# A latest start in the planner for conversions and operands that a one-core Trainium2 kernel makes ahead

## Chip, core and metric

The kernel runs on one core of one Trainium2 chip. The metric is the device time of one execution in microseconds; lower is better. Before the change the median of three runs is 877.93 us (876.68 to 880.76).

## What is computed

A layer of attention with a sigmoid in place of the softmax, followed by two feed-forward blocks. The shapes are 4 x 12 heads of 448 x 64, 1792 tokens, model width 768, and inner widths 768 and 2048.

```python
def _attn_ref(q, k, v):                  # (4, 12, 448, 64)
    scores = scale * np.matmul(q, k.transpose(0, 1, 3, 2)) - np.log(S)
    attn = 1.0 / (1.0 + np.exp(-scores))
    return np.matmul(attn, v).astype(np.float32)

def _moe_ref(x, w1, w2, w3, w_out):      # x: 1792 x 768, all weights 768 x 768
    h = np.maximum(np.maximum(x @ w1, x @ w2), x @ w3)
    return (h @ w_out).astype(np.float32)

def _moe2_ref(x, w_in, w_out):           # w_in 768 x 2048, w_out 2048 x 768
    h = x @ w_in
    g = h * (1.0 / (1.0 + np.exp(-1.702 * h)))
    return (g @ w_out).astype(np.float32)
```

All products run in float32 precision, and the weights arrive as 64-bit floats, which the kernel itself turns into 32-bit ones.

## The kernel before

**Stages, in order of TensorE's work.** Attention over 24 pairs of heads ("couples"), in twelve double steps; the first feed-forward block for tokens of two batches at a time, as layer 1 (first pass), layer 2 (first pass), layer 1 (second pass, the other two batches), layer 2 (second pass); then the second block, in groups of its inner width (`tp, fp`, lines 886 to 901), and a tail.

**Products.** A 2 x 2 block product is done with seven products in place of eight (the sums of blocks are made in `moving` for the activations and in `Weights.steps` for the weights; `Set.step` places the seven). Each factor is split into a rounded part and a rest (`split`, line 382: a cast and a subtraction), and a product of 384 in depth is three blocks times three matmuls: nine matmuls of 448 columns, `product`, line 484, issued at line 492. The planner counts 9 x 0.201 us for it. A `stage` (line 536) runs the sets of a layer interlocked, 9 x 7 = 63 steps in layer 1 and 3 x 7 in layer 2.

**Weights, and what is made ahead.**
- `single` (line 346) turns one 128 x 768 tile of 64-bit weights into 32-bit ones: a load of 768 KB (line 353), on ScalarE L357 (the high word) and L362 (the low bits; in attention this part is on VectorE, L364), on VectorE L367, L368 and L372. The raw words go into one of two places, `raw_at`, in turn (some take a third place); the result into one of four places, `y_at`.
- `prepare` (line 665) and `prepare4` (line 671) call it long before the tile is used and write the result to DRAM (`yk`, `y4`). 18 are declared in attention (`convert`, line 679), 6 beside the first pass of layer 1, 16 beside the second pass, and 16 beside the first four groups of the second block (lines 896 to 900): 56 in all.
- `Weights.operand` (line 469) makes one operand of a product: at its first use it is split from the 32-bit tile into a slot of a ring of nine (`w_at`) and written to DRAM (`kept`); later uses load it from `kept`. In the second pass of layer 1 four of the nine sets (`REDO`) make their operands anew.
- The list `extra` (lines 773 to 783) holds what the second pass of layer 1 does beside its own work, 24 pieces: 8 `prepare`, 8 `prepare4`, and for the first pair of tiles of the second block a reload of `yk` (`Weights(12, ...)`) and its seven operands, each with a split and a write to `kept`. Their order is: tile pair 12 (two), the reload, seven operands, two `prepare4`, then four conversions for each of the next three pairs. `stage` declares piece j after step floor(63j/24) + 1.

**What sets the order of work.** Nothing runs where it is written. Every operation is declared to `Order` (line 88) with the places in memory that it reads and writes, so its predecessors follow; `Order.run` (line 126) then makes a plan on the host and issues the instructions in that order on TensorE, VectorE, ScalarE and SP (which issues all DMAs). On the chip each engine takes its instructions strictly as issued, and semaphores hold them.

The planner has two passes. Backward, each operation gets `late`, the latest start that delays nobody: the smallest `late` of its successors minus its own cost and a lag (0.1 us, after a DMA 1.0 us, after a raw load 2.0 us). TensorE's operations have a fixed `at`: `O.clock`, the sum of TensorE's planned work that was declared before them. Forward, each engine that is free takes, of the operations that are ready, the one with the smallest `late`:

```python
            late = min((x.late - took - o.lag for x in o.post), default=1e9)
            o.late = late if o.at is None else min(late, o.at)
...
                heapq.heappush(ready[e], (o.late + (SLACK if e == "DVE" and len(o.on) > 1 else 0.0), o.n, o))
```

Planned costs are those of lines 48 to 57 (768 columns: 0.84 us on ScalarE, 0.96 or 0.56 us on VectorE), 1.95 us for L362, and for a DMA its size over 350 KB/us plus 2.0 us and the lag. A conversion, whose reader is a reload far behind, so has a `late` that can lie far behind the place where it is declared; its only other bounds are the buffers it shares with later work.

Of the kernel before, what the change touches and what calls it, by code (L numbers as in the profile page):

```python
# [186 lines left out]
T = S  # L187
# [12 lines left out]
EARLY = 4  # L200
LEAD = 2
READY = 1
REDO = (1, 3, 5, 7)


def moe_chain_kernel(tc, qk, vv, wa, wb, out):
# [3 lines left out]
    O = Order()  # L210
# [36 lines left out]
    def F(at, n):  # L247
        if at >= FAR2:
            return Reg(sn4, at - FAR2, n, lambda: slab_n[3][:, at - FAR2 : at - FAR2 + n])
        if at >= FAR:  # L250
            return Reg(sn1, at - FAR, n, lambda: slab_n[0][:, at - FAR : at - FAR + n])
        return Reg(sf, at, n, lambda: slab_f[:, at : at + n])
# [38 lines left out]
    def dma(to, of, kb, reads=None, writes=None):  # L291
        return O.op(
            {"SP": kb / BUS},
            lambda e: sp.dma_start(to().bitcast(F32), of().bitcast(F32)),
            [of] if reads is None else reads,
            [to] if writes is None else writes,
        )
# [27 lines left out]
    XA, XB = 0, FAR  # L325
# [24 lines left out]
    def single(of, y, low_on, at=None, after=()):  # L350
        at = raw_at() if at is None else at
        raw = F(at, 2 * DM)
        O.op({"SP": 768 / BUS}, lambda e: sp.dma_start(raw().bitcast(mybir.dt.uint64), of), (), [raw], after, lag=LAND_RAW)
        half = lambda n: words(raw(), U16, n)
        u = lambda: y().bitcast(U32)
        by = dict(op0=ALU.bitwise_and, op1=ALU.bitwise_or)
        on("ACT", t_act(DM), lambda: act.activation(y(), words(raw(), F32, 1), AF.Copy, scale=2.0**-112), [raw], [y])  # L357
        byte = lambda: words(raw(), U8, 4)

        def low(e):  # L360
            if e == "ACT":
                act.activation(byte(), words(raw(), U32, 0), AF.Copy, scale=LOW)  # L362
            else:
                dve.tensor_scalar(half(2), half(1), 13, None, op0=ALU.logical_shift_right)  # L364

        O.op({low_on: 1.95 if low_on == "ACT" else 1.02}, lambda _: low(low_on), [raw], [raw])
        on("DVE", t_one(DM), lambda: dve.tensor_scalar(y(), y(), -TOP, TOP, op0=ALU.max, op1=ALU.min), [y], [y])  # L367
        on("DVE", t_one(DM), lambda: dve.tensor_scalar(u(), u(), 3, None, op0=ALU.logical_shift_left), [y], [y])  # L368
        on(
            "DVE",  # L370
            t_two(DM),
            lambda: dve.scalar_tensor_tensor(u(), words(raw(), U32, 1), 0x80000007, u(), **by),  # L372
            [y, raw],
            [y],
        )
# [49 lines left out]
    def tensors(i):  # L425

        if i < 9:
            return [(wa, 3 * m + i % 3) for m in (i // 3, i // 3 + 3)]
        if i < 12:
            return [(wa, 18 + m) for m in (i - 9, i - 6)]  # L430
        return [(wb, 4 * (i - 12) + n) for n in range(2)]
# [52 lines left out]
    def product(ps, w, x, fresh):  # L484
# [15 lines left out]

        O.pe(f, 9 * MM, [*w, *(z for p in parts for z in p)] + ([] if fresh else [ps]), [ps])

    def temp():
        return F(temp_at(), T)

    class Set:


        def __init__(self, x, weights, put, bank, temp=temp):
            self.x, self.weights, self.put, self.bank, self.temp = x, weights, put, bank, temp  # L510
# [25 lines left out]
    def stage(sets, extra=()):  # L536
        steps = sorted((7 * i + 2 * n, i, n) for i in range(len(sets)) for n in range(7))
        done = 0
        for k, (_, s, n) in enumerate(steps):
            sets[s].step(n)  # L540
            while done * len(steps) < (k + 1) * len(extra):
                extra[done]()
                done += 1


# [119 lines left out]
    def prepare(i, n, low="DVE", at=None, after=()):  # L665
        of, t = tensors(i)[n]
        y = F(y_at() if at is None else at + 2 * DM, DM)
        single(of[t], y, low, at, after)
        dma(yk[i][1](n), y, 384)

    def prepare4(f, low):
        y = F(y_at(), DM)
        single(wb[tile4(f)], y, low)
        dma(y4[f], y, 384)

    def tile4(f):
        return f % 8 * 4 + 2 + f // 8

    def convert(c):
        p = c.p - LEAD  # L680
        if 0 <= p < 18:
            prepare(p // 2, p % 2, at=XA + 12 * T if c.p % 3 == 2 else None, after=[c.load])

    prev, last = None, None
    for i in range(NP // 2):
        x = Couple(2 * i)
        x.values()
        if i == 0:
            x.score(0, slice(0, 1))
            x.score(1, slice(0, 1))  # L690
            x.score(0, slice(1, 3))
            x.scored(0)
            x.score(1, slice(1, 3))
            x.scored(1)
        for n in range(0 if i else 2, 3):
            x.score(n)
            x.scored(n)
        convert(x)
        if prev:
            weigh_last(prev, last)  # L700
        y = Couple(2 * i + 1)
        y.values()
        last = sigmoid(score_last((x, y)))
        for n in range(3 if prev else 0):
            prev[1].weigh(n)
        for n in range(3):
            y.score(n)
            y.scored(n)
        convert(y)
        for n in range(3):  # L710
            x.weigh(n)
        prev = (x, y)
# [12 lines left out]
    def layer1(x, first, base, extra=()):  # L725
        sets = []
        for m in range(HK):
            for e in range(3):

                def put(half, tok, ps, other, m=m, e=e):  # L730
                    to = pairs(base, half, tok, m)
                    if e == 0 and other is None:
                        copy(to, ps, S, psum=True)
                        return
                    if other is not None:
                        new = to if e == 0 else temp()
                        add(new, ps, other, S)
                        ps = new
                    if e:
                        two(to, ps, to, ALU.max, S)  # L740

                def weights(i=3 * m + e):
                    if first or i not in REDO:
                        return Weights(i, first, sums(), keep=i not in REDO)
                    at = again()
                    return Weights(i, True, at + 2 * DM, y=at, keep=False)

                sets.append(Set(x, weights, put, ps_at))
        stage(sets, extra)
# [3 lines left out]
    def layer2(h, first, base):  # L753
        sets = []
        for m in range(HK):

            def put(half, tok, ps, other, m=m):
                to = temp() if base is None else pairs(base, half, tok, m)
                if other is None:
                    copy(to, ps, S, psum=True)  # L760
                else:
                    add(to, ps, other, S)
                dma(zk[base is not None][half][tok][1](m), to, 224)

            sets.append(Set(h, lambda m=m: Weights(9 + m, first, sums()), put, ps_at))
        stage(sets)
# [6 lines left out]
    extra = []  # L773
    for fp in range(EARLY):
        for n in range(2):
            extra.append(lambda fp=fp, n=n: prepare(12 + fp, n, "ACT"))
        if fp < READY:
            w = []
# [22 lines left out]
    class Group:  # L801


        def __init__(self, fp, tp, z):
            self.fp, self.tp, self.g, self.w = fp, tp, {}, None
            first = self.first = (tp == 1) == (fp < PAIRS // 2)
            early = self.early = fp < EARLY or fp >= PAIRS // 2
            self.set = Set(z, lambda: Weights(12 + fp, first and fp >= READY, s3, early), self.put, b3)
            self.at = None
# [68 lines left out]
    half = PAIRS // 2  # L878

    def reload(tp):  # L880
        for side in range(2):
            for tok in range(2):
                dma(F(raw0 + (6 * side + 3 * tok) * T, 3 * T), zk[tp][side][tok][0], 672)
        return moving(raw0, t=s3, at=zslots)
# [3 lines left out]
    for tp, fp in [(1, n) for n in range(half)] + [(0, n) for n in range(PAIRS)]:  # L888
        if (tp, fp) == (0, 0):
            z = reload(0)  # L890
        g = Group(fp, tp, z)
        for n in range(7):
            g.set.step(n)
            for i in range(2 * n - 2, 2 * n) if before and n else ():
                before.unit(i)
        if tp == 0 and fp < half:
            for n in range(2):
                prepare(12 + half + fp, n, "ACT")
            for n in range(2):
                prepare4(half + fp + 8 * n, "ACT")  # L900
        before = g


# [11 lines left out]
    def put3(half, tok, ps, other, k):  # L915
        g = F(G[2 * half + tok] + k * T, T)
        if other is not None:
# [4 lines left out]
        two(g, ps, sg, ALU.mult, S)  # L922

    stage(
        [
            Set(
# [205 lines left out]
```

## Time and profile before

| | |
|---|---|
| median of three runs | 877.93 us |
| profiled execution, its own time | 878.68 us |
| its span in the profile | 876.5 us |
| granted TensorE clock | full speed in all 40 slices |
| TensorE matmul, busy | 864.5 us (99%), 4558 instructions |
| weight loads, busy | 747.7 us (85%) |
| VectorE, busy | 690.0 us (79%), 1107 instructions |
| ScalarE, busy | 503.0 us (57%), 731 instructions |
| DMA | 238.13 MB, 272 GB/s in the mean |

How to read it: the profiler's span is that of one execution, and the execution's own time is 2.2 us longer. PE is TensorE, PEld its weight loads, DVE VectorE, ACT ScalarE, SP the engine that issues DMAs (SPq is its queue). The names of tiles are the program's: f, n, m and r are the four slabs of on-chip memory, ps the accumulators, yk, y, kept, z and spill are in DRAM, in_wb and in_wa are the raw weights. `f<-in_wb` reads "f is written from in_wb". Ends of matmuls are modelled by the profiler, so the waits of the weight loads tell more of TensorE's holes than its busy time. Planned times (`O.clock`, `late`) are the planner's own and not times of the device.

### The profile page before, as it was taken

Reading aid. Unit: us, or ns where it says so; the run is one execution under the profiler, and the core shown is the slowest. Engines: PE = TensorE matmul, PEld = TensorE weight load, DVE = VectorE, ACT = ScalarE, POOL = GpSimd, SP = SyncE. Lnnn points to the kernel's source line nnn. Section 1 sums busy time; section 2 is a strip of 40 time slices with the busy share of each in tenths; the row PEclk is TensorE's granted clock in tenths of the full one; section 3 lists DMA queues with packets and bytes.
Section 4 is the critical chain, followed back from the end, with each engine's and each line's share of the span. In section 5 each row is a group of like instructions: output and inputs, shape, how many; then the busy total and the mean of one; then the engine's idle time right before and its main releaser. Section 6 shows DMA issues by size and latency. Waiting matters only on the chain.

```text
span 876.5 us, 12583 instructions
## 1 busy us (share of the span) xinstructions
PE 864.5 (99%) x4558; PEld 747.7 (85%) x4558; DVE 690.0 (79%) x1107; ACT 503.0 (57%) x731; POOL 1.1 (0%) x6
## 2 busy tenths in 40 slices
PE   9999999999999989999999999999999999999998
PEld 5544448999998978999989999999999999999997
DVE  5888898878899877778697888756688888753894
ACT  7887887556566545566566444665665444423540
POOL 0000000000000000000000000000000000000000
PEclk9999999999999999999999999999999999999999
DMA  8899977777839988888989956998768674686113
GB/s 300 299 317 326 373 248 240 248 257 248 290 153 375 366 314 298 277 298 297 395 349 385 367 167 196 388 354 321 276 247 303 251 276 148 217 283 199 31 64 126
DMA packets 77533, 238.13 MB, mean 272 GB/s; under 512 B 8608, under 2 KB 18208, under 8 KB 77472
## 3 DMA queue, kind: packets, MB, share of 16 engines
q1 hardware_dynamic: 77472, 237.34, 76.5%
q8 instruction: 36, 0.59, 0.2%
q14 instruction: 25, 0.20, 0.1%
HBM read 151.19 MB, written 86.11 MB: 271 GB/s over the span
## 4 chain that ended last, share of the span: by engine, by line
PE 94%; DVE 4%; DMA 1%; ACT 1%; issue 1%; POOLq 0%; DVEq 0%; POOL 0%; ACTq 0%
PE ps L492 53%; PE ps L859 7%; PE ps L858 7%; PE ps L860 7%; PE ps L602 7%; PE ps L1000 6%; PE ps L583 6%; DVE f L312 2%; DVE r L312 1%; PE ps L646 1%; PE ps L635 1%; DMA kept<-r 1%; PE ps L662 0%; DVE m L312 0%; ACT r L309 0%
## 5 line engine op out<-in xcount | busy, mean ns | idle before, releaser
L492 PE MATMUL ps<-r 128*128 128x448 f32 x2250 | 465.8, 362 | 4.2 <-DVE f L312 2.3
L492 PEld LDWEIGHTS ps<-r 128*128 128x128 f32 x2250 | 421.3, 188 | 35.6 <-DVE f L312 1.9
L312 DVE TENSOR_TENSOR f<-ps,f 128x448 f32<-128x448 f32 x214 | 132.5, 623 | 90.8 <-PE ps L860 35.4
L312 DVE TENSOR_TENSOR r<-f,r 128x384 fp32r<-128x384 f32 (+3 forms) x252 | 160.7, 660 | 11.2 <-ACT r L309 10.1
L309 ACT CAST r<-f 128x384 fp32r<-128x384 f32 (+3 forms) x206 | 113.7, 580 | 66.0 <-PE ps L492 30.5
L309 ACT COPY f<-ps 128x448 f32<-128x448 f32 x124 | 66.5, 540 | 109.5 <-PE ps L492 75.8
L312 DVE TENSOR_TENSOR f<-f 128x384 f32<-128x384 f32 (+2 forms) x189 | 121.3, 659 | 9.1 <-ACT f L921 4.1
L618 ACT ACTIVATE m<-ps,bias 128x896 f32<-128x896 f32 x84 | 78.8, 1007 | 11.4 <-PE ps L583 10.0
L362 ACT ACTIVATE f<-f 128x768 uint8<-128x768 uint32 x38 | 74.8, 1968 | 0.6
L357 ACT ACTIVATE f<-f 128x768 f32<-128x768 f32 x56 | 51.2, 915 | 17.7 <-DMA f<-in_wb 9.5
L492 PE MATMUL ps<-m,r 128*128 128x448 f32 x270 | 58.4, 363 | 1.4 <-DVE r L309 1.1
L602 PE MATMUL ps<-m,f 128*64 128x448 f32 x288 | 59.4, 548 | 0.0
L372 DVE SCALAR_TENSOR_TENSOR f<-f 128x768 uint32<-128x768 uint32 x56 | 53.2, 954 | 4.9 <-ACT f L362 4.4
L583 PEld LDWEIGHTS ps<-r 64*128 64x128 f32 x432 | 39.3, 187 | 19.1 <-ACT m L618 9.2
L492 PEld LDWEIGHTS ps<-m,r 128*128 128x128 f32 x270 | 50.4, 187 | 5.7 <-DVE r L309 1.5
L583 PE MATMUL ps<-r 64*128 64x448 f32 x432 | 50.7, 376 | 0.0
L602 PEld LDWEIGHTS ps<-m,f 128*64 128x64 f32 x288 | 18.5, 136 | 34.4 <-issue 31.7
L309 ACT COPY ps<-ps 128x448 f32<-128x448 f32 x43 | 23.2, 539 | 31.9 <-PE ps L492 28.8
L309 ACT CAST m<-f 128x448 fp32r<-128x448 f32 (+4 forms) x36 | 26.1, 724 | 23.9 <-DVE f L312 15.8
L312 DVE TENSOR_TENSOR n<-f,n 128x448 fp32r<-128x448 f32 (+4 forms) x51 | 37.9, 745 | 1.7 <-ACT n L309 1.1
L367 DVE TENSOR_SCALAR f<-f 128x768 f32<-128x768 f32 x56 | 31.1, 555 | 8.2 <-ACT f L357 8.0
L312 DVE TENSOR_TENSOR m<-f,m 128x448 fp32r<-128x448 f32 (+4 forms) x41 | 34.0, 832 | 4.1 <-ACT m L309 4.0
(81 smaller groups left out, 896.1 us busy)
## 6 DMA issues: line engine op xcount, KB each, us to landing
r<-kept SPq DMA_DIRECT2D x119, 384.0 KB, 4.9
kept<-r SPq DMA_DIRECT2D x112, 384.0 KB, 5.2
f<-in_wb SPq DMA_DIRECT2D x32, 768.0 KB, 7.1
f<-in_wa SPq DMA_DIRECT2D x24, 768.0 KB, 6.9
f<-yk SPq DMA_DIRECT2D x24, 768.0 KB, 5.5
yk<-f SPq DMA_DIRECT2D x40, 384.0 KB, 6.8
f<-y SPq DMA_DIRECT2D x24, 384.0 KB, 5.4
f<-in_qk SPq DMA_DIRECT2D x15, 456.0 KB, 5.8
```

The source lines that it names most:

```text
L309: return O.op(engines, lambda e: (act.copy if e == "ACT" else dve.tensor_copy)(to(), of()), [of], [to])
L312: return on("DVE", t_two(n), lambda: dve.tensor_tensor(to(), a(), b(), op=op), [a, b], [to])
L362: act.activation(byte(), words(raw(), U32, 0), AF.Copy, scale=LOW)
L372: lambda: dve.scalar_tensor_tensor(u(), words(raw(), U32, 1), 0x80000007, u(), **by),
L492: pe.matmul(o, a[:, c], b, start=fresh and j == n == 0, stop=j == HK - 1 and n == 2, skip_group_check=True,)
L583: pe.matmul(o[:, e, :], kx[r, c * P : (c + 1) * P], qx[r, Q:QK], start=n == 0, stop=n == 2)
L602: pe.matmul(o[r], w[:, 2 * c + e], x[:, e * S : (e + 1) * S], start=begin, stop=end)
L618: lambda: act.activation(a().rearrange("p (e s) -> p e s", e=2), ps(), AF.Sigmoid, bias=bias, scale=scale),
L858: pe.matmul(ps(), wh[:, c], gh, start=fresh and j == 0, **how)
L859: pe.matmul(ps(), wh[:, c], gl, start=False, **how)
L860: pe.matmul(ps(), wl[:, c], gh, start=False, stop=j == 1, skip_group_check=True)
L1000: pe.matmul(o, a, b, start=fresh and k == n == 0, stop=k == 3 and n == 2, skip_group_check=True)
```

## The change

A constant, `AHEAD = 5.5`, and a helper, `soon`, are added. `soon(f)` runs `f` and then gives every operation that `f` declared `at = O.clock + AHEAD`; in the planner's backward pass its `late` is then at most that. The four places that declare work made ahead go through it: the 24 pieces of `extra` in the second pass of layer 1 and the 6 in the first pass (both in `stage`), `convert` in attention, and the conversions beside the first groups of the second block. No operation is added or taken away, and TensorE's own `at` values stay as they were.

```diff
@@ -200,6 +200,7 @@
 EARLY = 4
 LEAD = 2
 READY = 1
+AHEAD = 5.5
 REDO = (1, 3, 5, 7)
 
 
@@ -500,6 +501,13 @@
 
         O.pe(f, 9 * MM, [*w, *(z for p in parts for z in p)] + ([] if fresh else [ps]), [ps])
 
+    def soon(f):
+
+        n = len(O.ops)
+        f()
+        for o in O.ops[n:]:
+            o.at = O.clock + AHEAD
+
     def temp():
         return F(temp_at(), T)
 
@@ -539,7 +547,7 @@
         for k, (_, s, n) in enumerate(steps):
             sets[s].step(n)
             while done * len(steps) < (k + 1) * len(extra):
-                extra[done]()
+                soon(extra[done])
                 done += 1
 
 
@@ -679,7 +687,7 @@
     def convert(c):
         p = c.p - LEAD
         if 0 <= p < 18:
-            prepare(p // 2, p % 2, at=XA + 12 * T if c.p % 3 == 2 else None, after=[c.load])
+            soon(lambda: prepare(p // 2, p % 2, at=XA + 12 * T if c.p % 3 == 2 else None, after=[c.load]))
 
     prev, last = None, None
     for i in range(NP // 2):
@@ -895,9 +903,9 @@
                 before.unit(i)
         if tp == 0 and fp < half:
             for n in range(2):
-                prepare(12 + half + fp, n, "ACT")
+                soon(lambda: prepare(12 + half + fp, n, "ACT"))
             for n in range(2):
-                prepare4(half + fp + 8 * n, "ACT")
+                soon(lambda: prepare4(half + fp + 8 * n, "ACT"))
         before = g
 
 
```

## Rows read from the trace of the kernel before

**Rows 1.** The profile page: busy time, share and instructions of each engine.
```profile
PE 864.5 (99%) x4558; PEld 747.7 (85%) x4558; DVE 690.0 (79%) x1107; ACT 503.0 (57%) x731; POOL 1.1 (0%) x6
```

**Rows 2.** Stretches (first: L492 alone): us, PE, PEld, DVE, ACT, POOL, clock, DMA, GB/s.
```profile
133.50:287.50 154.00, 153.21 (x764) 143.07 (x765) 1.00 0.73 261
...
100.00:125.00 25.00, 25.00 (x186) 12.17 (x184) 23.31 (x33) 21.67 (x26) 0.00 (x0) 1.00 0.87 295
...
600.00:625.00 25.00, 25.00 (x125) 23.26 (x124) 17.88 (x31) 15.85 (x18) 0.00 (x0) 1.00 0.83 297
...
300.00:316.00 16.00, 16.00 (x82) 14.99 (x81) 10.62 (x21) 6.21 (x10) 0.00 (x0) 1.00 0.82 273
...
338.00:400.00 62.00, 62.00 (x312) 58.12 (x311) 49.42 (x84) 37.64 (x46) 0.00 (x0) 1.00 0.82 274
...
440.00:462.00 22.00, 20.32 (x101) 18.36 (x99) 21.27 (x34) 14.49 (x28) 0.00 (x0) 1.00 0.87 337
```

**Rows 3.** Waits of weight loads, 300 to 340 us, then 440 to 462 us.
```profile
PEld ps L492 <- DVE f L312: 1.9, 1, 1.9
PEld ps L492 <- DVE r L309: 1.5, 1, 1.5
PEld ps L492 <- DVE n L312: 1.1, 1, 1.1
PEld ps L492 <- DVE r L312: 0.9, 2, 0.6
...
PEld ps L492 <- ACT ps L309: 1.5, 1, 1.5
PEld ps L859 <- DVE m L312: 0.9, 1, 0.9
```

**Rows 4.** DMA issues of 282–284, of 301.3–301.9, and of 278–340 us.
```profile
f<-in_wb SPq DMA_DIRECT2D x1, 768.0 KB, 9.5
...
yk<-f SPq DMA_DIRECT2D x1, 384.0 KB, 8.1
...
f<-in_wb SPq DMA_DIRECT2D x6, 768.0 KB, 7.7
kept<-r SPq DMA_DIRECT2D x10, 384.0 KB, 7.2
```

**Rows 5.** Timeline, 295 to 327 us, of the tile, its reload and the writes.
```profile
295.06 0.91 ACT L357 ACTIVATE f<-f 128x768 f32<-128x768 f32 x1
...
301.42 0.51 SPq L294 DMA_DIRECT2D yk<-f  x1
...
308.96 0.93 SPq L294 DMA_DIRECT2D f<-yk  x2
...
317.17 4.13 SPq L294 DMA_DIRECT2D kept<-r  x5
...
323.38 0.93 ACT L309 CAST r<-f 128x384 fp32r<-128x384 f32 x2 [3.35 <-DMA kept<-r]
```

**Rows 6.** Groups of instructions of a conversion: busy us, mean ns, idle before.
```profile
L362 ACT ACTIVATE f<-f 128x768 uint8<-128x768 uint32 x38 | 74.8, 1968 | 0.6
...
L372 DVE SCALAR_TENSOR_TENSOR f<-f 128x768 uint32<-128x768 uint32 x56 | 53.2, 954 | 4.9 <-ACT f L362 4.4
L357 ACT ACTIVATE f<-f 128x768 f32<-128x768 f32 x56 | 51.2, 915 | 17.7 <-DMA f<-in_wb 9.5 <-DMA yk<-f 4.2 <-issue 2.3
...
L367 DVE TENSOR_SCALAR f<-f 128x768 f32<-128x768 f32 x56 | 31.1, 555 | 8.2 <-ACT f L357 8.0
```

**Rows 7.** Timeline, the last L372 of this pass; then L357 alone, 400–440 us.
```profile
437.68 0.95 DVE L372 SCALAR_TENSOR_TENSOR f<-f 128x768 uint32<-128x768 uint32 x1
...
400.00:440.00 40.00, 3.65 (x4) 1.00 0.96 353
```

**Rows 8.** Waits over the whole span: us in total, times, longest us.
```profile
ACT f L309 <- PE ps L492: 75.8, 69, 3.7
...
ACT f L357 <- DMA f<-in_wb: 9.5, 8, 4.2
```

## The prediction

> **What bounds the kernel now.** I read the page first: TensorE is busy for 864.5 us, 99% of the span [rows 1], but matmul ends are modelled, so I then read the table by stretch. In 600 to 625 us 125 matmuls start in 25 us, 0.2 us each and 1.8 us for a product of nine; that is the pace without a hole. The stretches 100 to 125 and 300 to 316 us show TensorE full as well, while VectorE is at 23.31 of 25 us in the first [rows 2]. Third, the waits of the weight loads, which show real holes: 1.9 + 1.5 + 1.1 + 0.9 = 5.4 us between 300 and 340 us, and 1.5 + 0.9 = 2.4 us between 440 and 462 us [rows 3]. So TensorE sets the time, and work on other engines counts only where one of these holes opens, closes or is added.
>
> Last, the timeline of the first holes; it shows work made ahead that came late. The second pass of layer 1 begins near 285.9 us: by 287.5 us 764 matmuls of L492 had started [rows 2], 756 of them (12 sets of 63) belong to the passes before, and the other 8 take 1.6 us. Extra j of 24 is declared after step floor(63j/24) + 1, 1.8 us a step. The conversion "12, second tile" (j=1, step 3) is declared near 291.3 us, the first operand made ahead (j=3, step 8) near 300.3 us, the next at 305.7, 311.1, 314.7 and 320.1 us. What happened: the tile's load, issued between 282 and 284 us, took 9.5 us [rows 4], so it landed near 292.5; L357 ran at 295.06; the write to yk was issued at 301.42 and took 8.1 us [rows 4, 5]; the reload that needs it was held in SP's queue until 308.96; and five of the seven kept writes went out in one run from 317.17 us [rows 5]. A ring slot is free only when its kept write has landed: at 323.38 us ScalarE had sat 3.35 us for one [rows 5], and TensorE sat behind it. VectorE made the splits of that run in one go, which is the first of the holes (VectorE f).
>
> **The change, part by part.** It adds no instruction and removes none; it changes only what is picked first. 56 conversions (seven operations each, two of them DMAs), one reload and seven operands (25 operations), 418 in all, get a latest start of C + 5.5 us, C being the declared place. For a conversion the planner then works back with its own costs: write C + 5.5, L372 C + 4.4, L357 C + 2.2, load C - 2.0. No wait is added by hand. But each of the 418 can now be put ahead of other work in one of four in-order queues: ScalarE (evacuations, sigmoids, casts behind it), VectorE (sums and splits behind it), and SP, where 56 loads, 56 writes and 8 more DMAs pass kept reads.
>
> *Second pass of layer 1, the early operands.* The conversion's chain on ScalarE and VectorE is 0.915 + 1.968 + 0.954 = 3.84 us [rows 6] (L367 and L368 run beside L362). From 292.5 us it can end at 296.4, in time for the deadline of 291.3 + 5.5 = 296.8; before, its write went out at 301.42. So the write goes out 5 us sooner, the reload near 304.5, the first kept write near 312. There only operands 0 to 2 have been declared, and the later ones have deadlines 3.6 to 5.4 us apart, so the run of five is broken up. Operand 0's ring slot is wanted nine operands later, about 12 us after 300.3, so near 312. Its write landed near 317.17 + 7.2 = 324.4 [rows 4, 5], 12 us late, and would land near 319.2, 7 us late. In 300 to 316 us TensorE was full [rows 2], and its first hole opens only after 318: products of the other set covered some 6 us of lateness. 7 - 6 = 1 us is left of the 5.4. **Minus 4.4.** Ends: minus 2.3 if the wait only shrinks in proportion (5.4 x 5/12), minus 5.4 if it goes whole; I take the value near the upper end, since the full stretch is the nearest row.
> A rule reads this otherwise. The Trainium skill, "DMA: Bandwidth & Descriptors", section on the anatomy of one DMA, gives about 2.0 us fixed plus the bytes over 436 GB/s, for the gpsimd path. That is an estimated 2.9 us for a 384 KB write, the whole 5.4 would go, and the sum below would be minus 6.2. The 8.1 and 7.2 us of the rows on SP's queue decide against it.
>
> *Second pass, the later conversions.* The sixteenth is declared at step 61, near 402 us with the holes, yet a last L372 ran at 437.68 us. Four L357 started between 400 and 440 us [rows 7]. Their work comes forward into a stretch that has ScalarE at 37.64 and VectorE at 49.42 of 62 us [rows 2]: plus 4 x 2.88 = 11.5 and 4 x (2 x 0.555 + 0.954) = 8.3 us [rows 6], L368 having the form of L367, make 49 and 57.7, 79% and 93%. The 93% is the level of 100 to 125 us, which has no hole. Zero, covered by that; ends minus 0.5 and plus 2.9 (one ScalarE pair fully uncovered).
>
> *The passage at 440 to 462 us.* There VectorE works 21.27 of 22 us [rows 2], on the next operands above all, and a conversion's three operations (2.06 us) stand right before it [rows 7]. Gone from there, the chain may start up to 2.1 us sooner, of which ScalarE and TensorE's own results take back most. **Minus 0.8**, a third of the 2.4; ends minus 2.4 and plus 0.5.
>
> *Attention, the first layer-1 pass and the second block.* 18, 6 and 16 conversions run there already beside a full TensorE [rows 2]; they move by a few us up to some tens. Zero each. If the cover is gone: in attention one L357 before an awaited sigmoid costs 0.915 [rows 6], plus 3.7 for four of 18; in the second block a pair of 2.88 us minus the 1.1 us that an evacuation waits for TensorE on average (75.8 / 69) [rows 8], plus 1.8 for each of four groups, 7.1. Below zero: minus 0.7 in all.
>
> Sum: minus 4.4 minus 0.8 = minus 5.2 us. The profiled run took 878.68 us (span 876.5), 0.75 above the median 877.93; it would take 873.5, and the median **872.7 us**, 0.6% less. A measurement of this kernel tells about 0.5%, 4.4 us, from no change.
>
> **Rivals.** *A, the round trip stays (no change).* The DMA share, not the order, holds the reload: loads of 7.7 and kept writes of 7.2 us median between 278 and 340 us [rows 4] get no faster, and conversions pulled ahead crowd the same stretch, so the proportional end holds and nothing is won at 440. Minus 2.3 plus a hole of 0.5 elsewhere: 876.1 us. For: the two landings of 8.1 and 9.5 us were most of the delay. Against: 5 us of it was waiting for a turn. In this case falls also that the change does little, because most conversions already ran in idle time.
>
> *B, conversions hold ScalarE's queue (slower).* The order is fixed beforehand with a planned landing of 2.2 + 2.0 + 2.0 = 6.2 us, while loads took 7.7 [rows 4]. A conversion with an early deadline is put right behind its planned landing, and ScalarE then stands 1.5 us with copies and sigmoids behind it; before, far-off due times put most L357 later than that. It stood 9.5 us in 8 such waits, up to 4.2 [rows 8], which a TensorE full on both sides hid. Beyond the 1.1 us of slack 0.4 to 0.6 us would reach TensorE for each of the 32 in_wb conversions. The gain is eaten from 9 to 13 of them on; if all 32 pay 0.4 = 12.8 us, the time is 872.7 + 12.8 = 885.5, with two thirds of them 881. Against: eight such waits cost no hole that rows 3 shows.
> On this the Trainium skill, "Perfetto Trace Analysis", section on per-engine timelines, says that ScalarE and VectorE keep strict first-in, first-out order. By that rule one late load stops every evacuation behind it and the time would be B's; the waits on in_wb agree with the mechanism, their harmlessness speaks against the price.
>
> **How the numbers follow.** Forecast (gain of at least 4.4): 0.48. A (between a gain of 4.4 and a loss of 4.4): 0.38. B (loss above that): 0.14. The range takes in the upper ends (5.4 + 2.4 + 0.5 + 0.7 = 9.0, so 869) with 1 us beyond them, and reaches through A to a small loss: 868 to 880. About 0.12 of B and little below is left out; gains alone would span 868 to 873.5.
>
> **What would show it.** Right: the second tile's write to yk near 296 us, its reload before 306, kept writes of operands in runs of three at most, weight-load waits of 300 to 340 us at 1 to 2 us instead of 5.4, no L357 between 410 and 440 us. Wrong: the reload still near 309, or new waits of weight loads in attention, in 340 to 440 or in 550 to 650 us; for B more than 20 us of ScalarE's L357 waiting for in_wb, with TensorE idle right after. A time above 876 would say that the order of picks was not what opened the holes.

## The result and the profile after

The changed kernel takes 869.68 us (median of six runs, 869.09 to 870.58). The kernel before, with three more runs beside it, has a median of 878.21 over its six. The ratio is 0.9899 with a 95% interval of 0.9882 to 0.9916: 1.0% faster, 8 to 9 us. The prediction was 872.7 us in a range of 868 to 880; the direction and the mechanism it put first were right, the gain was larger than its sum of 5.2 us.

The page after; compare [rows 1], and for L358 the line of L357 in [rows 6] (the new code moves L357 to L358, L492 to L493 and so on):

```profile
span 868.1 us, 12632 instructions
...
PE 862.0 (99%) x4558; PEld 748.5 (86%) x4558; DVE 684.6 (79%) x1095; ACT 508.9 (59%) x743; POOL 1.1 (0%) x6
...
L358 ACT ACTIVATE f<-f 128x768 f32<-128x768 f32 x56 | 51.0, 915 | 1.0 <-DVE r L313 0.8
```

The same 4558 matmuls are done. ScalarE no longer stands for a load ahead of a conversion: 1.0 us of idle time before the 56 L358, where it was 17.7 us, 9.5 of them for in_wb [rows 6, 8].

Where the 8 us came from shows in the table by stretch: us, then busy time and instructions of PE, PEld, DVE, ACT, POOL, then clock, DMA share, GB/s. First the kernel before, in three stretches that the rows ahead of the prediction do not have:

```profile
250.00:275.00 25.00, 24.21 (x121) 22.15 (x120) 24.86 (x44) 14.50 (x29) 0.00 (x0) 1.00 0.75 281
...
300.00:325.00 25.00, 23.46 (x115) 21.07 (x114) 18.21 (x37) 10.64 (x19) 0.00 (x0) 1.00 0.89 293
325.00:350.00 25.00, 22.93 (x113) 20.48 (x112) 17.99 (x36) 12.82 (x18) 0.00 (x0) 1.00 0.85 315
```

Then the changed kernel:

```profile
250.00:275.00 25.00, 25.00 (x127) 23.43 (x126) 22.80 (x39) 14.62 (x29) 0.00 (x0) 1.00 0.78 294
...
300.00:325.00 25.00, 25.00 (x127) 23.43 (x126) 18.65 (x37) 13.58 (x24) 0.00 (x0) 1.00 0.98 355
325.00:350.00 25.00, 25.00 (x127) 23.44 (x126) 20.72 (x40) 15.51 (x19) 0.00 (x0) 1.00 0.83 304
```

The reader is to see the counts: 121, 115 and 113 matmuls became 127 each, which is 6 + 12 + 14 = 32 more, at 0.2 us some 6.4 us. TensorE is full from attention to 444 us. What is left behind attention are waits of weight loads in two places, from 436 to 460 us (2.4 us in [rows 3]) and after 760 us:

```profile
PEld ps L493 <- ACT f L310: 1.0, 1, 1.0
...
PEld ps L866 <- DVE f L313: 0.6, 1, 0.6
```

The timeline of the tile pair that the prediction followed answers to [rows 5]:

```profile
263.57 0.40 SPq L354 DMA_DIRECT2D f<-in_wb  x1
271.75 0.33 SPq L354 DMA_DIRECT2D f<-in_wb  x1
...
282.07 0.92 ACT L358 ACTIVATE f<-f 128x768 f32<-128x768 f32 x1
...
290.73 0.32 SPq L295 DMA_DIRECT2D yk<-f  x1
...
298.92 0.38 SPq L295 DMA_DIRECT2D f<-yk  x1
...
309.82 3.00 SPq L295 DMA_DIRECT2D kept<-r  x4
...
314.03 1.47 SPq L295 DMA_DIRECT2D kept<-r  x2
```

The second tile's load goes out at 271.75 us (the second line). For the kernel before, two lines of the same timeline belong beside it:

```profile
282.80 0.49 SPq L353 DMA_DIRECT2D f<-in_wb  x1
...
309.58 0.32 SPq L294 DMA_DIRECT2D f<-yk  x1
```

The first is the tile's load. The second is its reload: [rows 5] show two reloads merged at 308.96, and the tile's write of 301.42 took 8.1 us [rows 4], so it landed at 309.5 and only the second of the two can read it. The first is one of those that the sets of `REDO` need. So the load goes out at 271.75 instead of 282.80 us, the write at 290.73 instead of 301.42, the reload at 298.92 instead of 309.58, now ahead of that other one, and the first kept writes at 309.82 instead of 317.17. From write to reload it is 8.2 us in both kernels: the round trip did not get shorter, it starts sooner.

### The profile page after: what moved, and what is told of

Read it like the earlier page. It is cut to its first block, busy times and chain, and to the rows that moved or that the text cites. A ratio compares the mean times of both kernels' runs of the same rounds, so it can differ in the third digit from the quotient of the medians.

```text
span 868.1 us, 12632 instructions
## 1 busy us (share of the span) xinstructions
PE 862.0 (99%) x4558; PEld 748.5 (86%) x4558; DVE 684.6 (79%) x1095; ACT 508.9 (59%) x743; POOL 1.1 (0%) x6
## 4 chain that ended last, share of the span: by engine, by line
PE 98%; DVE 1%; DMA 1%; SPq 0%; issue 0%; POOLq 0%; ACT 0%; DVEq 0%; POOL 0%
PE ps L493 58%; PE ps L610 7%; PE ps L866 6%; PE ps L867 6%; PE ps L868 6%; PE ps L1008 6%; PE ps L591 6%; PE ps L654 1%; PE ps L643 1%; DMA out_t<-f 1%; PE ps L670 0%; SPq L295 0%; DVE f L959 0%; DVE r L313 0%; DVE f L313 0%
## 5 line engine op out<-in xcount | busy, mean ns | idle before, releaser
L493 PE MATMUL ps<-r 128*128 128x448 f32 x2250 | 465.0, 362 | 0.6 <-ACT f L310 0.6
L493 PEld LDWEIGHTS ps<-r 128*128 128x128 f32 x2250 | 421.7, 187 | 30.4 <-ACT f L310 1.0
L313 DVE TENSOR_TENSOR r<-f,r 128x384 fp32r<-128x384 f32 (+3 forms) x252 | 161.3, 660 | 19.2 <-ACT r L310 17.7
L310 ACT CAST r<-f 128x384 fp32r<-128x384 f32 (+3 forms) x214 | 120.3, 591 | 43.0 <-PE ps L493 26.6
L310 ACT COPY f<-ps 128x448 f32<-128x448 f32 x128 | 68.8, 540 | 120.2 <-PE ps L493 89.9
L493 PE MATMUL ps<-m,r 128*128 128x448 f32 x270 | 57.7, 362 | 0.0
L493 PEld LDWEIGHTS ps<-m,r 128*128 128x128 f32 x270 | 50.6, 187 | 3.4
L358 ACT ACTIVATE f<-f 128x768 f32<-128x768 f32 x56 | 51.0, 915 | 1.0 <-DVE r L313 0.8
L368 DVE TENSOR_SCALAR f<-f 128x768 f32<-128x768 f32 x56 | 31.1, 555 | 9.7 <-ACT f L358 9.6
```

What stands on the lines that cost most here:

```text
L310: return O.op(engines, lambda e: (act.copy if e == "ACT" else dve.tensor_copy)(to(), of()), [of], [to])
L313: return on("DVE", t_two(n), lambda: dve.tensor_tensor(to(), a(), b(), op=op), [a, b], [to])
L493: pe.matmul(o, a[:, c], b, start=fresh and j == n == 0, stop=j == HK - 1 and n == 2, skip_group_check=True,)
```

## Experiments: one place at a time

`soon` is used in four places. Four kernels keep the deadline in one place each and call the work plainly in the other three, as in

```diff
-                soon(extra[done])
+                (soon if ahead else lambda f: f())(extra[done])
...
-                soon(lambda: prepare(12 + half + fp, n, "ACT"))
+                prepare(12 + half + fp, n, "ACT")
```

Three theories stood: each hole is closed by the work declared next to it (1); the second pass can come early only when the first pass's conversions are out of the way (2); every conversion that moves gives a share (3).

**The second pass of layer 1 alone.** Expected:

> Only the 24 pieces beside the second pass of layer 1 get the deadline. Theory 1 (each hole is closed by the work declared next to it): the holes of 300 to 340 us go and the one at 445 shrinks, about 6.5 us faster, no hole left between 300 and 440; the holes near 90 and 245 to 264 us stay. Theory 2 (cascade: the pieces of this pass can only come early when the first pass's conversions are out of the way): 2 to 4 us faster, some 2 us of weight-load waits left between 300 and 340. Theory 3 (every conversion that moves gives its share): 16 of 56 conversions, about 2.4 us.

Measured: 872.52 us against 877.47, ratio 0.9944 (0.9932 to 0.9956), 4.9 us faster. Of the weight-load waits between 300 and 436 us 0.4 us is left, the one near 445 is 1.0 us, those of 240 to 270 stay at 1.3. So the place is enough to close these holes by itself, against theory 2, with 1.5 us less gain than theory 1 gave; a new wait of 1.8 us on a kept load, at 288 us, is about of that size.

**The first pass of layer 1 alone.** Expected:

> Only the six conversions beside the first pass of layer 1 get the deadline. Theory 1: the waits of 240 to 270 us (1.3 us) go and nothing else, about 1.2 us faster, the holes of 300 to 340 us stay at 5 to 6 us. Theory 2: as theory 1, but the first loads for the second pass also move ahead of 278 us and a part of the 5.8 us goes: 2 to 3 us faster. Theory 3: 0.9 us.

Measured: 871.79 us, ratio 0.9937 (0.9925 to 0.9949), 5.7 us faster, more than any theory had. The holes of 240 to 270 go, and so do those of 300 to 340, though nothing in the second pass has a deadline. The timeline of this kernel shows the same tile pair again, earlier by itself (the first of the two reloads is the tile's):

```profile
297.20 0.36 SPq L295 DMA_DIRECT2D yk<-f  x1
...
302.58 2.90 SPq L295 DMA_DIRECT2D f<-yk  x2
...
310.20 1.80 SPq L295 DMA_DIRECT2D kept<-r  x3
...
313.38 1.42 SPq L295 DMA_DIRECT2D kept<-r  x2
```

Here the write goes out 4.2 us sooner than before, and it also lands faster, in 3.9 us instead of 8.1. From 288 to 300 us the DMA engines moved 282 GB/s in this kernel and 399 before.

**Attention alone, and the second block alone.** Expected:

> Only the 18 conversions in attention get the deadline. Theory 1: the one wait near 90 us (0.7 us) goes, 0.7 to 0.9 us faster, all later holes as before. Theory 2: the same. Theory 3: 2.7 us faster.

> Only the 16 conversions beside the first four groups of the second block get the deadline. Theory 1 and 2: no hole was there, no change within 0.5 us. Theory 3: 2.4 us faster. If conversions ahead hold ScalarE's queue (rival B of the prediction): slower by 1 to 7 us, with waits of weight loads between 550 and 650 us.

Measured: attention 876.70 us, ratio 0.9991 (0.9982 to 0.9999), 0.8 us by the medians; the second block 877.32, ratio 1.0002 (0.9989 to 1.0015), nothing. Theory 3 falls: 34 of the 56 conversions give almost nothing. The wait near 90 us was no steady hole either: the kernel of the second pass alone, whose attention has no deadlines, shows no such wait of TensorE in attention, and the one with attention's deadlines shows 1.1 us there. What does shrink in the profile of attention alone are the weight-load waits between 240 and 270 us, from 1.3 to 0.6 us.

## Experiments: which pieces of the second pass

Three kernels set the deadline for some of the 24 pieces of the second pass and nowhere else:

```diff
+                (soon if ahead and done < 2 else lambda f: f())(extra[done])
...
+                (soon if ahead and 2 <= done < 10 else lambda f: f())(extra[done])
...
+                (soon if ahead and done >= 10 else lambda f: f())(extra[done])
```

> Of the 24 pieces only the two conversions of tile pair 12 get the deadline. If the 300 to 340 us holes come from the late yk round trip of this pair (the prediction's reading): its second write near 295, the reload near 303, the holes of 300 to 340 gone, 4 to 5 us faster, the hole near 445 as before. If it is the burst of the seven operands that matters: 0 to 1.5 us, holes stay.

> Of the 24 pieces only the reload and the seven operands get the deadline. Round-trip reading: the reload's due time moves 1.5 us at most and pulls the two conversions by as much, so 0 to 1.5 us faster with most of the 5.8 us of weight-load waits left. Burst reading: the holes go, 4 to 5 us faster.

> Of the 24 pieces only the later 14 conversions get the deadline. Expected: holes of 300 to 340 us stay; no conversion is left between 410 and 440 us and the hole near 445 shrinks, 0.5 to 1.5 us faster. If the late conversions have nothing to do with the passage at 440 us: no change. If crowding VectorE to 93% between 340 and 400 us costs: slower by up to 2 us.

Measured: tile pair 12 alone 871.96 us, ratio 0.9933 (0.9916 to 0.9950), 5.4 to 5.9 us faster; the reload and the operands 876.56, ratio 0.9988 (0.9974 to 1.0002); the later 14 conversions 877.07, ratio 0.9997 (0.9982 to 1.0012). Two conversions carry the whole of what this place is worth, and 22 other pieces nothing that can be told. Of the timelines, tile pair 12 alone first (its reload is the first of the two):

```profile
292.99 0.36 SPq L295 DMA_DIRECT2D yk<-f  x1
...
300.82 4.68 SPq L295 DMA_DIRECT2D f<-yk  x2
```

then the operands alone, with the run of five kept writes as before (here the tile's reload is the second of the two, at 304.19 us: the write took 6.2 us to land):

```profile
297.94 0.43 SPq L295 DMA_DIRECT2D yk<-f  x1
...
302.31 2.20 SPq L295 DMA_DIRECT2D f<-yk  x2
...
314.19 3.94 SPq L295 DMA_DIRECT2D kept<-r  x5
```

and this kernel's one weight-load wait between 300 and 340 us:

```profile
PEld ps L493 <- DVE n L313: 2.9, 1, 2.9
```

The operands' deadline pulls the pair with it by way of the planner's backward pass, 3.5 us in the write, and half of the weight-load waits go; yet the time hardly moves. In the profiled execution two things take back the 2.9 us. The first is the clock, behind this one wait (the matmuls, then TensorE alone in the 3.4 us that follow: us, busy time and instructions, granted clock, DMA share, GB/s):

```profile
319.88 3.62 PE L493 MATMUL ps<-r 128*128 128x448 f32 x9 [2.53 <-DMA r<-kept]
```

```profile
319.90:323.30 3.40, 3.40 (x10) 0.51 0.69 277
```

After TensorE had stood for 2.5 us the granted clock was at its lower level, 1.2 GHz, until 323.3 us, and ten matmuls started 0.37 us apart instead of 0.2: some 1.6 us. No other profile of these runs has such a stretch between attention and the last matmuls. The second is that the waits between 436 and 466 us are 3.7 us instead of 2.4, of which 2.0 stand at 459.7 us. The later conversions alone leave the tile's reload at 310.54 us and 4.8 us of waits. Between 340 and 400 us, where VectorE was to reach 93%, no hole opened in any of the runs: the price of 0 to 2.9 us was rightly taken as nothing. The waits near 445 us are 1.0 us in that kernel, but only 0.3 in the one of tile pair 12, which moves none of the later conversions. That hole changes with every order of work, and its cause is not settled by these runs.

## Experiments: why the first pass mattered, and whether the cures add up

After the first runs a fourth theory: VectorE. It works at 20 to 22 of 25 us in the first pass, and in the passage to layer 2, from 250 to 275 us, at 24.86 of 25. What the late conversions take from it before the passage is work for the passage put off; the holes open there, all that follows is some us late, tile pair 12 with it, and so the holes near 320 us. All deadlines but those of the second pass:

> All deadlines but those of the second pass of layer 1. Since the first pass's deadlines alone closed the holes of 300 to 340 us too, theory 4 (VectorE's backlog at the passage near 250 us delays all that follows, tile 12 with it, and either cure is enough): 6 to 6.5 us faster, the same as the first pass's plus attention's, with 2 to 3 us of waits left near 445. If the cures add up: 4 us or less faster with holes left between 300 and 340.

Measured: 871.19 us against 877.38, ratio 0.9925 (0.9908 to 0.9942), 6.2 us faster, with 0.3 us of waits left between 300 and 340 and 1.9 between 436 and 466. The first pass gives 5.7, the second pass 4.9, attention 0.8, together 11.4; the whole change gives 8.5. They share the holes of 300 to 340 us.

Then two kernels without any deadline, which leave out a part of the six conversions of the first pass (`skip`): one the three VectorE operations, L367, L368 and L372, the other ScalarE's L362. Of the edit, the lines that do it:

```diff
-        O.op({low_on: 1.95 if low_on == "ACT" else 1.02}, lambda _: low(low_on), [raw], [raw])
+        if skip != "ACT":
+            O.op({low_on: 1.95 if low_on == "ACT" else 1.02}, lambda _: low(low_on), [raw], [raw])
+        if skip == "DVE":
+            return
```

> The kernel before, but the six conversions beside the first pass of layer 1 leave out their three VectorE operations (L367, L368 and L372), 6 x 2.06 = 12.4 us of VectorE between 140 and 231 us; the rest is the same and no deadline is set. Theory 4 (VectorE's backlog, put off work of the passage near 250 us, makes the hole there and delays tile 12): the hole of 240 to 270 us goes, tile 12's write and reload come 4 to 6 us earlier, most of the 5.8 us of waits in 300 to 340 go, 4 to 6 us faster, about as the deadlines of the first pass alone. If it is their place in SP's queue or ScalarE: no more than 1 us faster.

> The kernel before, but the six conversions beside the first pass of layer 1 leave out ScalarE's L362 (6 x 1.97 = 11.8 us of ScalarE). Theory 4: ScalarE had room there, within 1 us of before, the holes of 240 to 270 and of 300 to 340 us stay. If ScalarE's load is what delays: 4 to 6 us faster.

Measured: without VectorE's part 871.27 us against 877.02, ratio 0.9932 (0.9913 to 0.9952); without ScalarE's 877.03, ratio 1.0001 (0.9992 to 1.0010). The stretch of 256 to 264 us shows it, in the columns above: first the kernel before, then the first pass's deadlines alone, then without VectorE's part, then without ScalarE's:

```profile
256.00:264.00 8.00, 7.51 (x38) 6.66 (x36) 8.00 (x14) 4.75 (x9) 0.00 (x0) 1.00 0.70 256
```

```profile
256.00:264.00 8.00, 8.00 (x42) 7.50 (x41) 7.11 (x13) 3.63 (x7) 0.00 (x0) 1.00 0.96 333
```

```profile
256.00:264.00 8.00, 8.00 (x42) 7.50 (x41) 6.98 (x13) 3.20 (x8) 0.00 (x0) 1.00 0.97 334
```

```profile
256.00:264.00 8.00, 7.79 (x40) 6.99 (x39) 6.62 (x13) 3.84 (x8) 0.00 (x0) 1.00 0.93 312
```

VectorE is at 8.00 of 8.00 us before. With 12.4 us of its work taken out, or with the conversions merely done sooner, it has idle time here and TensorE none. Without VectorE's part the tile's reload goes at 302.05 us, and 0.4 us of waits is left between 300 and 340. With 11.8 us taken from ScalarE TensorE's hole here becomes smaller too, the weight-load waits between 240 and 270 us fall from 1.3 to 0.5, but the reload goes at 307.73 and 5.5 us of waits stay between 300 and 340, and the time stays. So it is VectorE's part of the late conversions that counts, and not ScalarE's. The planner orders the work anew in each kernel, so no single order is tested.

The link is in VectorE's timeline before the passage. Of the sums for the passage's factors that are two blocks wide (`f<-f 128x896`), the first behind 205 us ran at 233.34 us in the kernel before:

```profile
230.62 0.96 DVE L372 SCALAR_TENSOR_TENSOR f<-f 128x768 uint32<-128x768 uint32 x1
...
233.34 1.08 DVE L312 TENSOR_TENSOR f<-f 128x896 f32<-128x896 f32 x1
```

and at 214.52 us with the first pass's deadlines alone, where the last conversion had ended by 203.5:

```profile
214.52 1.08 DVE L313 TENSOR_TENSOR f<-f 128x896 f32<-128x896 f32 x1
...
226.23 1.09 DVE L313 TENSOR_TENSOR f<-f 128x896 f32<-128x896 f32 x1
```

Theory 4 puts this down to VectorE's time. A rival that no kernel parts from it is a place in memory. The raw words of these six conversions lie at `XA + 12 * T` (line 769), and the first sum of the passage is written to the same place (`t = base + 12 * T`, line 404), so in any plan the sum has to follow the last conversion's last use of it. Without ScalarE's L362 the two stand 0.4 us apart (L372 is L375 there):

```profile
225.62 0.96 DVE L375 SCALAR_TENSOR_TENSOR f<-f 128x768 uint32<-128x768 uint32 x1
...
226.96 1.08 DVE L312 TENSOR_TENSOR f<-f 128x896 f32<-128x896 f32 x1
```

Without VectorE's part the last use is L362, over at 196.3 us, and the sum comes about when it does with the deadlines:

```profile
194.31 2.00 ACT L362 ACTIVATE f<-f 128x768 uint8<-128x768 uint32 x1
...
213.99 1.08 DVE L312 TENSOR_TENSOR f<-f 128x896 f32<-128x896 f32 x1
```

And in the kernel before, VectorE was not full while the sum waited, 13.14 of 16.10 us:

```profile
214.50:230.60 16.10, 16.10 (x82) 15.09 (x81) 13.14 (x25) 9.07 (x14) 0.00 (x0) 1.00 0.82 295
```

So leaving out VectorE's part both took work away and set the place free 35 us sooner (196.3 instead of 231.6). The rows speak for the place as what holds the sum back; a kernel with the raw words elsewhere and no deadline would settle it, and none was run.

Nor is the delay of tile pair 12 only lateness handed on. The second pass starts (matmul 757 of L492) at 285.98 us before, at 284.33 without L362 and at 283.98 with the first pass's deadlines alone; the tile's reload comes 23.6, 23.4 and 18.6 us behind that start. With the deadlines the write goes out 2.2 us sooner against it and lands 4.2 us faster; why it lands faster is not shown.

## Experiments: an earlier deadline, and a leaner set

```diff
-AHEAD = 5.5
+AHEAD = 0.0
```

> The changed kernel with a deadline of C + 0 in place of C + 5.5. If conversions ahead of other work hold ScalarE's or VectorE's queue (rival B), the more so the earlier they are due: slower than the changed kernel by 2 to 6 us, 872 to 876 us, with holes in attention or in 340 to 440 us. If any early deadline does (they wait for their loads and buffers anyway): 869 to 871 us, as with 5.5.

Measured: 871.14 us against 877.02, ratio 0.9929 (0.9917 to 0.9942). That is nearer to 870 than to 876: an early deadline does no great harm. It is a little behind 5.5 (medians of 871.14 and 869.68; the kernel before had 877.02 beside the one and 878.21 beside the other), and its profile has one hole that the changed kernel lacks, between 300 and 340 us, for a copy of ScalarE:

```profile
PEld ps L493 <- ACT ps L310: 1.0, 1, 1.0
```

Whether that hole is the difference is open; the two profiles end TensorE's work within 0.1 us of each other.

The leaner set keeps the deadlines of attention, of the first pass and of tile pair 12:

```diff
+                (soon if ahead and (len(extra) == 6 or done < 2) else lambda f: f())(extra[done])
...
+                prepare(12 + half + fp, n, "ACT")
```

> The changed kernel with deadlines only where the runs showed a gain: attention, the six conversions of the first pass, and tile pair 12; the operands, the later 14 conversions and the second block have none. If the other 38 pieces do nothing: 869 to 870.5 us, as the changed kernel. If they cost what tile pair 12 alone won over all 24 (0.5 us): 869. If they close the hole near 445 (2.4 us before, 1.0 after): 870.5 to 871.5.

Measured: 869.81 us, ratio 0.9916 (0.9902 to 0.9931), the same as the changed kernel within both intervals. The other 38 pieces add nothing, and leaving them out gains nothing. In this profile the only weight-load wait between 130 us and the end that is not on issue or attention's operations is this one, near 445 us:

```profile
PEld ps L493 <- DVE r L313: 0.3, 1, 0.3
```

## Why the prediction was right, and where its sum was short

**The early operands: right, and undersized.** The term was minus 4.4 with an end of minus 5.4. The round trip of tile pair 12 was the cause: the two conversions alone give 5.4 to 5.9 us, of which the waits near 445 us, 0.3 instead of 2.4, may hold up to 2. The holes go with the time of the tile's reload: at 309.58, 310.54 and 307.73 us (before, later conversions alone, without L362) there are 5.8 (the 5.4 of [rows 3] and a small one of 0.4), 4.8 and 5.5 us of waits; at 304.19 (operands alone) 2.9; at 302 to 303 us 0 to 0.4 (four kernels); at 301 us or before none (tile pair 12 alone, the changed kernel, the leaner set; only the kernel with C + 0 has 1.3 us, for that copy above all). The kernels of attention and of the second block alone reload as late as before and have 5.3 and 5.7. The prediction read the wrong one of two reloads, 308.96, as the tile's; that was 0.6 us off and does not enter its sum. What was assumed too carefully: that the tile's load would still land near 292.5 us. The deadline on the chain moved the load most, to 271.75 instead of 282.80 us. The first kept write, foretold near 312, came at 309.82; the runs were of four and two, not of three at most.

**Zero for the first layer-1 pass: the step of the sum that failed.** The reason given was that TensorE is full beside these conversions. That looked at the stretch in which they ran. What they cost lay behind it, in the passage near 250 us, whose first sum came 19 us later for them and where VectorE is then full: alone this place gives 5.7 us. In the whole change most of that is the same holes of 300 to 340 us, closed twice over; its own part is the 1.3 us of weight-load waits between 240 and 270 us, which the prediction passed over. Attention's deadlines alone also bring those waits down, to 0.6. Whether VectorE's time or the shared place in memory holds the sum back stays open.

**The passage at 440 us: a size near enough, a cause not shown.** Minus 0.8 was taken; the waits there went from 2.4 to 1.0 us. As foretold, no L358 runs between 410 and 440 us in the changed kernel. But in the leaner set two do, at 413.35 and 417.16 us, and the wait there is only 0.3; and the later conversions alone moved the time by nothing measurable.

**Attention, the second block, the later conversions: zero, and close to zero they are:** 0.9991, 1.0002 and 0.9997, each with its whole interval within 0.2% of no change.

**Rival A** fell. The round trip of 8 us did stay in the changed kernel, as it said, but the chain could start 11 us sooner, at the load, and a sooner start was worth the whole of the holes. By the same rows the rule of the Trainium skill that was weighed ("DMA: Bandwidth & Descriptors", the anatomy of one DMA) gave the right sum for this term, all 5.4 us, by a wrong road: the tile's write took 7.9 us in the changed kernel, not the estimated 2.9. That is no fixed price either: a kept write of the same size, at 245.63 us, took 2.3.

**Rival B** fell at its first step. It wanted more than 20 us of ScalarE standing for in_wb ahead of L357; there is none, and 1.0 us of idle time before L358 for all causes. The deadline reaches the load first (C - 2.0 against C + 2.2 for the conversion), and the loads went out far ahead: tile pair 12's first load at 263.57 us and its L358 at 276.43, 12.9 us later, where it had been 8.5 us. The strict order of ScalarE's queue, of which the Trainium skill speaks ("Perfetto Trace Analysis", per-engine timelines), is not contradicted by any row here; what it needed to do harm, a conversion ahead of its load, did not come about.

The missing 3.3 us are thus some 1.4 us of the early operands (5.8 went, 4.4 taken), 1.3 us of the passage near 250 us, and 0.6 us more at 440 us, against a little given back elsewhere.

## What to carry to other kernels

In a list schedule a piece of work whose reader is far away has no pressure on it and runs where nobody else wants the engine, until its buffers force it in a burst; a due time near its place of declaration cost nothing that could be measured here, and brought it out of the way of the next dense stretch. To price moved work, look not at the stretch that it leaves but at the next one where the engine is full, at the places in memory that the work holds until then, and follow the round trips through memory that start from it. An experiment that leaves work out also frees what that work held: check both before naming one of them as the cause. Cures may overlap: test each alone and in the whole before adding up their gains.

## What was not expected

Making conversions due earlier took ScalarE's waits for loads away instead of adding to them (9.5 us for in_wb before, 4.0 in the kernel with a deadline of C + 0, none in the changed one). And 11.8 us of ScalarE's work taken out of the first pass moved the time by 0.0 us, while 12.4 us of VectorE's in the same place moved it by 5.8.
